# The first batch of an attention and expert kernel: the mask added by TensorE in PSUM instead of by VectorE, and a new order of that stage

## The chip, the cores and the metric

The kernel runs on one core of a Trainium2 chip. The metric is the time of one execution in device microseconds; for the kernel before it is the median of three runs. The profile is of one more execution of the same program, and its times count from the start of its span.

## The reference, cut to what matters

Four batches of attention with 8 heads, 576 positions and head size 64 feed two expert layers; the change is in the attention of batch 0.

```
scores = scale * np.matmul(q, k.transpose(0, 1, 3, 2))          # scale = 1 / 8
mask_plain = (rel >= 0) & (rel < 32)                            # heads 0 to 3
mask_dil = (rel >= 0) & (rel < 128) & (rel % 4 == 0)            # heads 4 to 7
scores = np.where(masks, scores, -1e9)
scores = scores - max(scores);  attn = exp(scores)
out = (attn / (sum(attn) + 1e-9)) @ v                           # (2304, 512) in all
x = max(out @ w1, out @ w2, out @ w3) @ w_out                   # moe, d_ff 768
...                                                             # moe2: 8 experts, d_ff 1024
```

## The kernel before, in words

The heads of a batch are done in four pairs, p = 0 to 3; pairs 2 and 3 are the dilated ones, with positions sorted so that their mask is a band too. For a pair the 576 query positions are nine tiles of 64; a tile's scores are 96 keys wide, and both heads of the pair stand above one another on 128 partitions. So a pair's scores are 128 x 864, in two PSUM banks of five and four tiles (480 and 384 columns).

A pair goes through steps, named by letters in a written order (`attn_ops`, from line 151): S computes the scores on TensorE (L181); Ma scales them and adds the mask on VectorE (L192), into SBUF (tile `sm`); Mb takes the maximum over each tile's keys, negated (L200). Pairs 0 and 2 are "fused": Xe is nine exponentials on ScalarE with the maximum as bias, each with its sum read out (L215). Pairs 1 and 3 aren't: Xs adds the maximum on GpSimd (L204), Xe is one exponential over 864 columns (L212), Xb sums on VectorE (L230). Ra adds 1e-9 to the sums and takes reciprocals (VectorE, L234 and L235), Rb multiplies by them (GpSimd, L238). T transposes the weights, three tiles in one group (TensorE, L249), E copies a group out of PSUM to SBUF (L253; a table says on ScalarE, A, or VectorE, V), V multiplies by v (TensorE, L266), one half at a time, H rounds the result to the first of two float parts (ScalarE, L286) and L subtracts to get the second (VectorE, L290). In a step's name the first digit is the pair, so T21 is group 1 of pair 2.

The inputs' weights `wm1` come as float64, as two 32-bit words, and are made into float32 by nine steps (`narrow_ops`, line 312): c1 takes the exponent (VectorE, L326), c2 moves it to its float32 place (ScalarE, L330), c3 puts the sign in (VectorE, L331), c4 masks the mantissa (VectorE, L334), c5 converts it (ScalarE, L337), c6 adds the low word (VectorE, L338), c7 multiplies (VectorE, L341), c8 rounds (ScalarE, L319), c9 subtracts (VectorE, L323). `g0`, `g1`, `g2` are 1 MB loads of such weights (L352), each worth two tiles of 512 columns. Here the second digit is the tile: c31 is c3 of tile 1. Tiles 0 and 1 come from `g0`, tile 2 from `g1`.

What sets the order: the loads of the stage go out on SP's queue in the order of `LOADS` (line 45; k is a pair's keys and queries, m a part of the mask, v the values, g weights). The steps follow `ORDER` (line 48) on every engine, each engine in order. Work that isn't in `ORDER` (the next weights, the gate's weights of `load_gate`, line 652, batch 1's loads) is put between by a scheduler at compile time. Batches 1 to 3 run later beside the expert layers by `STAGES` (line 42) and `LATE`, always fused; their TensorE work starts with L175, their VectorE work with L192. After the stage come the first expert layer's products (L419). The first batch's score tiles are in the pool `ps_a` for pairs 0 and 2 and in `ps_g` for pairs 1 and 3.

Of the kernel before, what the change touches and what calls it, by code (L numbers as in the profile page):

```python
# [9 lines left out]
F32 = mybir.dt.float32  # L10
# [31 lines left out]
STAGES = {0: "S Ma Mb Xs Xe Xb Ra Rb", 6: "W", 8: "T0 E0 T1 E1", 9: "T2 E2", 11: "V0 H0 L0 V1 H1 L1"}  # L42


LOADS = "k0 m0 k1 k2 m2 k3 v0 g0 v1 g1 v2 v3"
FUSED = "1010"
EVAC = "AAV VAA VAV AAA".split()
ORDER = (
# [52 lines left out]
def attention_moe(ctx: ExitStack, tc: tile.TileContext, q, k, v, mask, wm1, wg, wm2, out):  # L101
# [27 lines left out]
    mk = at_p.tile([P, BANK0 + NQ * KW], F32, name="mk", bufs=1)  # L129
# [21 lines left out]
    def attn_ops(b, p, pool, qt, kt, vt, fused, evac):  # L151
# [12 lines left out]
        def s():  # L164
            if b == 0 and p % 2:
# [14 lines left out]
            for t in range(0 if corners else NQ):  # L180
                nc.tensor.matmul(  # L181
                    h["s"][t // T0][:, (t % T0) * KW:(t % T0 + 1) * KW],
                    qt[:, t], kt[:, t * QT:t * QT + KW],
                    start=True, stop=True,
                )

        def ma():
            h["m"] = pool.tile([P, NQ, KW], F32, name="sm", bufs=2 if pool is at_p else 3)
            for a, (t0, t1) in enumerate(halves):
                n = (t1 - t0) * KW  # L190
                m0 = BANK0 + t0 * KW if dil else a * KW
                nc.vector.scalar_tensor_tensor(  # L192
                    out=h["m"][:, t0:t1].rearrange("p t k -> p (t k)"),
                    in0=h["s"][a][:, 0:n], scalar=1.0 / D ** 0.5, in1=mk[:, m0:m0 + n],
                    op0=ALU.mult, op1=ALU.add,
                )

        def mb():
            h["st"] = pool.tile([P, 3, NQ], F32, name="st")
            nc.vector.tensor_reduce(out=h["st"][:, 0], in_=h["m"], axis=AX.X, op=ALU.max, negate=True)  # L200

        def xs():
            if not fused:
                nc.gpsimd.tensor_tensor(  # L204
                    out=h["m"], in0=h["m"], in1=h["st"][:, 0].unsqueeze(2).to_broadcast([P, NQ, KW]),
                    op=ALU.add,
                )

        def xe():
            sm, st = h["m"], h["st"]  # L210
            if not fused:
                nc.scalar.activation(out=sm, in_=sm, func=AF.Exp)  # L212
                return
# [13 lines left out]

        def xb():
            if not fused:
                nc.vector.tensor_reduce(out=h["st"][:, 1], in_=h["m"], axis=AX.X, op=ALU.add)  # L230
# [61 lines left out]
        ops = {"W": w, "S": s, "Ma": ma, "Mb": mb, "Xs": xs, "Xe": xe, "Xb": xb, "Ra": ra, "Rb": rb}  # L292
# [19 lines left out]
    def narrow_ops(dst, bits, parts):  # L312
# [8 lines left out]
        def lo():  # L321
            for w, x in parts:
# [384 lines left out]
    for what in LOADS.split():  # L707
# [30 lines left out]
    assert not steps  # L738
    at0_p.release()
# [156 lines left out]
    def hooks(unit):  # L896
# [626 lines left out]
```

## Time and profile before

| what | us |
|---|---|
| median of three runs | 1898.69 (1898.12 to 1899.18) |
| the profiled execution, its own time | 1901.93 |
| its span in the trace | 1899.9 |
| TensorE busy | 1853.2 (98% of the span) |
| VectorE busy | 1341.1 (71%) |
| ScalarE busy | 976.6 (51%) |
| GpSimd busy | 651.3 (34%) |

In the profile PE is TensorE's matmuls and PEld its weight loads, DVE is VectorE, ACT ScalarE, POOL GpSimd, SPq the queue of SyncE that issues DMAs. A busy share is an average over the whole span. The first batch's stage takes the first 47 us of it.

### The profile page before, as it was taken

The page shows a single profiled execution, that of the slowest core. Times are in us where ns is not written, and L with a number is a line of the kernel's source. Part 1 is how long each engine was busy: PE and PEld are TensorE (multiplying, and loading weights), DVE is VectorE, ACT ScalarE, POOL GpSimd, SP SyncE. Part 2 cuts the span into 40 slices and gives each one's busy share as a digit, 9 for nine tenths or more (in the row PEclk, how much of TensorE's full clock was granted, in tenths as well). Part 3 has the DMA queues.
Part 4 walks back from the last instruction along what each step waited for, and adds up shares of the span by engine and source line. Part 5 has one row for each costly group of instructions (what it writes and reads, how often), then busy time and mean ns, then how long its engine had stood idle before and what let it go on. Part 6 is the DMA issues. An engine that isn't in the chain of part 4 may idle for free.

```text
span 1899.9 us, 34083 instructions
## 1 busy us (share of the span) xinstructions
PE 1853.2 (98%) x12051; PEld 1745.9 (92%) x12051; DVE 1341.1 (71%) x2529; ACT 976.6 (51%) x2362; POOL 651.3 (34%) x553
## 2 busy tenths in 40 slices
PE   7899999999999999999999999999999999999998
PEld 6899999998899987999999999999989999999997
DVE  7983364677866667666677777777777677876777
ACT  5663445444554444444456555565545555555554
POOL 2123243335666667666612121121211111211111
PEclk7899999999999999999999999999999999999999
DMA  7766486866667678766977767777798676676763
GB/s 262 277 217 222 151 274 202 304 226 228 237 252 259 252 252 291 263 254 250 363 257 235 237 218 225 239 233 237 232 331 262 211 233 225 225 255 212 234 219 100
DMA packets 218488, 458.81 MB, mean 241 GB/s; under 512 B 19920, under 2 KB 102992, under 8 KB 216784
## 3 DMA queue, kind: packets, MB, share of 16 engines
q1 hardware_dynamic: 216688, 454.29, 70.2%
q10 hardware_dynamic: 1632, 2.36, 0.4%
q8 instruction: 95, 1.56, 0.3%
q14 instruction: 73, 0.60, 0.1%
HBM read 325.76 MB, written 130.81 MB: 240 GB/s over the span
## 4 chain that ended last, share of the span: by engine, by line
PE 83%; DVE 8%; DMA 4%; ACT 2%; issue 1%; POOL 1%; DVEq 0%; SPq 0%; ACTq 0%; POOLq 0%
PE po L1292 25%; PE po L1387 12%; PE po L1037 10%; PE ps L419 7%; PE p L1387 6%; PE q L1387 6%; PE q L1083 4%; PE p L1083 4%; PE ps L629 4%; DMA raw<-in_wm 1%; PE ps L549 1%; DVE sums L771 1%; PE q L549 1%; DVE h L1135 1%; DVE ts L810 1%
## 5 line engine op out<-in xcount | busy, mean ns | idle before, releaser
L1292 PE MATMUL po<-wt,hop 128*128 128x256 f32 (+1 forms) x3264 | 482.9, 310 | 2.8 <-DMA wt<-wtd 2.8
L1292 PEld LDWEIGHTS po<-wt,hop 128*128 128x128 f32 x3264 | 444.9, 191 | 38.5 <-ACT wt L83 3.0
L84 POOL TENSOR_TENSOR wt<-raw,wt 128x256 fp32r<-128x256 f32 x192 | 186.2, 994 | 757.9 <-ACT wt L83 746.9
L84 DVE TENSOR_TENSOR hop<-r,hop 128x384 fp32r<-128x384 f32 x384 | 208.9, 574 | 188.3 <-ACT hop L83 184.7
L1037 PE MATMUL po<-wb,h 128*128 128x512 f32 x1152 | 295.2, 392 | 0.4 <-POOL wb L84 0.4
L1037 PEld LDWEIGHTS po<-wb,h 128*128 128x128 f32 x1152 | 213.6, 188 | 34.3 <-POOL wb L84 1.2
L83 ACT CAST hop<-r 128x384 fp32r<-128x384 f32 x384 | 188.7, 516 | 55.7 <-DVE r L1268 30.8
L419 PE MATMUL ps<-xt,wa 128*128 128x288 f32 x1296 | 187.7, 301 | 4.6 <-DVE wa L323 2.0
L419 PEld LDWEIGHTS ps<-xt,wa 128*128 128x128 f32 x1296 | 176.9, 191 | 8.2 <-DVE wa L323 2.3
L84 POOL TENSOR_TENSOR wa<-raw,wa 128x256 fp32r<-128x256 f32 (+1 forms) x107 | 129.8, 1217 | 111.9 <-ACT wa L83 91.0
L1401 ACT ACTIVATE r<-r 128x384 f32<-128x384 f32 x192 | 99.8, 525 | 128.9 <-DVE r L1400 128.0
L84 POOL TENSOR_TENSOR tw<-ts,tw 128x512 fp32r<-128x512 f32 x64 | 85.3, 1354 | 93.5 <-DVE h L1135 57.4
L1387 PE MATMUL po<-xB,wa 128*128 128x384 f32 x576 | 116.9, 338 | 0.0
L1387 PE MATMUL po<-xt,wa 128*128 128x384 f32 x576 | 116.9, 338 | 0.0
L1321 DVE SCALAR_TENSOR_TENSOR acc<-po,prob,acc 128x256 f32<-128x256 f32 x222 | 95.1, 476 | 21.9 <-PE po L1292 17.5
L84 POOL TENSOR_TENSOR wa<-sums,wa 128x512 fp32r<-128x512 f32 x64 | 88.7, 1404 | 53.3 <-ACT wa L83 28.4
L84 POOL TENSOR_TENSOR wb<-raw,wb 128x512 fp32r<-128x512 f32 x64 | 93.2, 1456 | 29.2 <-ACT wb L83 28.8
L1387 PEld LDWEIGHTS po<-xB,wa 128*128 128x128 f32 x576 | 102.5, 188 | 0.0
L1387 PEld LDWEIGHTS po<-xt,wa 128*128 128x128 f32 x576 | 102.5, 188 | 0.0
L1262 DVE TENSOR_TENSOR r<-r,r 128x384 f32<-128x384 f32 x128 | 93.1, 728 | 2.2
L771 DVE TENSOR_TENSOR sums<-raw 128x256 f32<-128x256 f32 x64 | 41.4, 646 | 71.1 <-DMA raw<-in_wm 71.1
L1303 ACT COPY mm<-po 128x256 f32<-128x256 f32 x144 | 49.6, 375 | 79.9 <-PE po L1292 79.9
(236 smaller groups left out, 3364.7 us busy)
## 6 DMA issues: line engine op xcount, KB each, us to landing
wa<-wsd SPq DMA_DIRECT2D x192, 512.0 KB, 4.4
wt<-wtd SPq DMA_DIRECT2D x256, 256.0 KB, 3.9
wsd<-wa SPq DMA_DIRECT2D x96, 512.0 KB, 3.4
raw<-in_wm SPq DMA_DIRECT2D x64, 512.0 KB, 4.3
wtd<-tw SPq DMA_DIRECT2D x128, 256.0 KB, 2.8
raw<-in_wm SPq DMA_DIRECT2D x128, 256.0 KB, 5.4
wa<-wsd SPq DMA_DIRECT2D x64, 256.0 KB, 4.7
cx<-in_wm SPq DMA_DIRECT2D x12, 1024.0 KB, 6.8
```

Of the source, the lines that this page charges most:

```text
L83: nc.scalar.copy(hi, src)
L84: sub.tensor_tensor(out=lo, in0=src, in1=hi.bitcast(F32), op=ALU.subtract)
L419: nc.tensor.matmul(ps, w[:, wi, kk], xt[:, xi, kk, n0:n0 + HB], start=(n == 0), stop=(n == 3 * KT - 1),)
L629: nc.tensor.matmul(ps, wo[f][:, wi, d2 * P:(d2 + 1) * P], hs[f][:, hi, a * HB:(a + 1) * HB], start=(f == 0 and n == 0), stop=(f == NF1 - 1 ...
L771: nc.vector.tensor_tensor(out=s[:, o], in0=x, in1=y, op=op)
L1037: nc.tensor.matmul(po, self.hs[f, j][:, hi, t * P:(t + 1) * P], self.ws[f][:, wi], start=(n + f + k == 0), stop=(n == NPAIR - 1 and f == 1 ...
L1083: nc.tensor.matmul(ps, wo[w][:, wi, kk], xo[x][:, xi, kk], start=(first and k == 0), stop=True if k == 5 else False, skip_group_check=not ...
L1262: nc.vector.tensor_tensor(out=r[o, n], in0=r[x, n], in1=r[y, n], op=op)
L1292: nc.tensor.matmul(self.ps[side, t][:, 0:x.shape[-1]], h[:, hi, t * P:(t + 1) * P], x, start=(first and i == 0), stop=(n == NPAIR - 1 and ...
L1321: nc.vector.scalar_tensor_tensor(out=a, in0=src, scalar=g, in1=a, op0=ALU.mult, op1=ALU.add)
L1387: nc.tensor.matmul(ps[k][side], wo[k][w][:, wi, kk], xo[x][:, xi, kk], start=(first and c == 0), stop=c == 5, skip_group_check=not first,)
L1401: nc.scalar.activation(out=r, in_=r, func=AF.Relu)
```

## The change

TensorE starts each bank of batch 0's scores with a matmul of 8 times the identity and the mask, and the score matmuls add to it. M then takes the maximum from PSUM, in two parts, and scales it by 1/8; X is nine exponentials that read PSUM, for all four pairs. Ma, Mb, Xs, Xe and Xb are gone from batch 0, Xs and Xb altogether. Only 64 partitions of the mask are loaded; its first part is copied to the matmul's type by ScalarE, its second by GpSimd (r2), and after the stage a DMA copies it to the other 64 partitions for later batches. The mask's first part is the first load, the gate's weights are loaded third, and `g0` stands ahead of pair 3's keys and queries. Pair 1's evacuations are all VectorE's, and pair 2's scores go to `ps_g` in place of pair 3's. c1 is one masking operation instead of a shift and a mask, with c2's factor to match. Batches 1 to 3 allocate their statistics tile in Ma rather than in Mb.

```diff
-STAGES = {0: "S Ma Mb Xs Xe Xb Ra Rb", ...
+STAGES = {0: "S Ma Mb Xe Ra Rb", ...
-LOADS = "k0 m0 k1 k2 m2 k3 v0 g0 v1 g1 v2 v3"
-FUSED = "1010"
-EVAC = "AAV VAA VAV AAA".split()
+LOADS = "m0 k0 w0 k1 k2 m2 g0 k3 v0 g1 v1 v2 v3"
+EVAC = "AAV VVV VAV AAA".split()
 ORDER = (
-    "S0 M0a S1 M0b X0s X0e M1a S2 M1b X1s M2a X0b M2b S3 X1e R0a X2s X2e X1b R0b M3a T01+1 R1a "
-    "T02 M3b R1b E01 c11 T00+2 c10 c21 X2b E02 X3s R2a c20 T12+1 c31 E00 c30 E12 T10+1 R2b X3e "
-    "c41 V01 c40 T11 E10 c51 V00 X3b c50 T22 E11 c12 H00 T21 R3a H01 V10 c61 c22 R3b E22 E21 "
-    "V11 H10 c32 T20 H11 c60 c71 T31 c42 E31 E20 c52 c70 L01 T30+1 L00 c81 T32 V20 c62 E30 c91 "
-    "E32 L10 V21 c80 L11 V30 H20 c72 H21 L20 V31 H30 L21 c90 H31 L30 c82 L31 c92"
+    "S0 M0 X0 S1 M1 r2 R0a R0b X1 S2 M2 c10 c11 T02+1 T01 E02 c20 c21 E01 R1a R1b T00+2 E00 S3 X2 "
+    "c30 c40 c31 V01 V00 M3 R2a R2b c41 c50 T10 T11 E10 E11 T12 E12 c51 H01 H00 V11 V10 c12 X3 c60 c70 c61 "
+    "c71 R3a R3b c22 L01 L00 T20 E20 T21 E21 T22 E22 c80 H11 c81 H10 V21 V20 c90 c32 c42 L11 L10 c91 "
+    "T30+1 E30 T31 E31 T32 E32 c52 H21 H20 c62 L21 c72 L20 V31 V30 H31 c82 H30 c92 L31 L30"
 )
...
-    mk = at_p.tile([P, BANK0 + NQ * KW], F32, name="mk", bufs=1)
+    mr = at_p.tile([P, BANK0 + NQ * KW], F32R, name="mk", bufs=1)
+    mk = mr.bitcast(F32)
+    mraw = at0_p.tile([QT, BANK0 + NQ * KW], F32, name="mraw", bufs=1)
+    eyes = const.tile([QT, P], F32R, name="eyes")
+    for c in range(0, P, QT):
+        nc.vector.tensor_scalar_mul(eyes[:, c:c + QT], ident[:QT, :QT], float(D ** 0.5))
...
+            for a, (t0, t1) in enumerate(halves if b == 0 else ()):
+                n, m0 = (t1 - t0) * KW, mask_at(a)
+                nc.tensor.matmul(
+                    h["s"][a][:, 0:n], eyes, mr[:QT, m0:m0 + n], start=True, stop=False, skip_group_check=True,
+                )
...
-                    start=True, stop=True,
+                    start=False, stop=True, skip_group_check=True,
...
+        def m():
+            weights()
+            for a, (t0, t1) in enumerate(halves):
+                nc.vector.tensor_reduce(
+                    out=h["st"][:, 0, t0:t1],
+                    in_=h["s"][a][:, 0:(t1 - t0) * KW].rearrange("p (t k) -> p t k", k=KW),
+                    axis=AX.X, op=ALU.max, negate=True,
+                )
+            nc.vector.tensor_scalar_mul(h["st"][:, 0], h["st"][:, 0], 1.0 / D ** 0.5)
+
+        def x():
+            for a, (t0, t1) in enumerate(halves):
+                for t in range(t0, t1):
+                    nc.scalar.activation(
+                        out=h["m"][:, t], in_=h["s"][a][:, (t - t0) * KW:(t - t0 + 1) * KW], func=AF.Exp,
+                        scale=1.0 / D ** 0.5, bias=h["st"][:, 0, t:t + 1], accum_out=h["st"][:, 1, t:t + 1],
+                    )
...
-                out=z, in0=high, scalar1=20, scalar2=0x7FF,
-                op0=ALU.logical_shift_right, op1=ALU.bitwise_and,
+                out=z, in0=high, scalar1=0x7FF00000, scalar2=None, op0=ALU.bitwise_and
             ),
-            "c2": lambda: nc.scalar.activation(out=z, in_=z, func=AF.Relu, scale=2.0 ** 23, bias=ebias),
+            "c2": lambda: nc.scalar.activation(out=z, in_=z, func=AF.Relu, scale=8.0, bias=ebias),
...
-            nc.sync.dma_start(mk[:, m0:m1], mask[:, m0:m1])
+            nc.sync.dma_start(mraw[:, m0:m1], mask[:QT, m0:m1])
+            if i == 0:
+                nc.scalar.copy(mr[:QT, m0:m1], mraw[:, m0:m1])
+        elif what[0] == "w":
+            nc.sync.dma_start(wgr, wg)
...
+    steps = {"r2": lambda: nc.gpsimd.tensor_copy(mr[:QT, BANK0:], mraw[:, BANK0:])}
...
+    nc.sync.dma_start(mk[QT:, :], mk[:QT, :])
```

## Rows read from the trace of the kernel before

**Rows 1.** The page's first part: busy us, share, instructions.
```profile
PE 1853.2 (98%) x12051; PEld 1745.9 (92%) x12051; DVE 1341.1 (71%) x2529; ACT 976.6 (51%) x2362; POOL 651.3 (34%) x553
```
**Rows 2.** Busy time by stretch: length; busy per engine; clock, DMA share, GB/s.
```profile
7.07:20.37 13.30, 10.12 (x71) 9.45 (x71) 10.37 (x17) 7.96 (x38) 3.94 (x3) 0.87 1.03 358
20.37:47.25 26.88, 18.29 (x196) 15.06 (x196) 26.81 (x52) 17.63 (x38) 7.82 (x5) 0.68 0.65 212
47.25:90.00 42.75, 36.34 (x350) 33.76 (x349) 42.75 (x65) 27.42 (x74) 4.30 (x2) 0.88 0.74 272
90.00:120.00 30.00, 27.34 (x313) 25.86 (x312) 28.21 (x49) 24.32 (x75) 4.04 (x2) 1.00 0.66 231
```
**Rows 3.** The chain of waits, first 62 us: start, us, what.
```profile
1.19 4.04 DMA qt<-in_q
...
5.25 9.98 DMA qt<-in_q
...
20.46 2.92 DVE raw L326 x2
...
57.22 1.85 PE ps L419 x12
```
**Rows 4.** The issue of the first weights' load at 7.6 us, and its landing.
```profile
L352 SPq DMA_DIRECT2D cx<-in_wm x1: 347/347/347, 7.6 to 7.6; - x1
...
DMA to landing us min/median/max: 12.0/12.0/12.0
```
**Rows 5.** Groups by form, first 48 us: busy us, mean ns | idle before, releasers.
```profile
L238 POOL TENSOR_TENSOR sm<-sm,st 128x864 f32<-128x864 f32 x4 | 7.1, 1764 | 8.3 <-DVE st L235 7.4 <-ACT sm L212 0.9
L215 ACT ACTIVATE sm<-sm,st 128x96 f32<-128x96 f32 x18 | 6.5, 360 | 7.6 <-DVE st L200 7.6
...
L331 DVE SCALAR_TENSOR_TENSOR raw<-cx,raw 128x512 uint32<-128x512 uint32 x4 | 4.9, 1250 | 0.0
...
L200 DVE TENSOR_REDUCE st<-sm 128x9 f32<-128x864 f32 x4 | 4.2, 1040 | 0.1
...
L326 DVE TENSOR_SCALAR raw<-cx 128x512 uint32<-128x512 uint32 x4 | 3.7, 976 | 0.0
...
L338 DVE SCALAR_TENSOR_TENSOR cx<-cx 128x512 f32<-128x512 uint32 x4 | 2.7, 668 | 0.0
...
L319 ACT CAST wa<-raw 128x512 fp32r<-128x512 f32 x4 | 2.5, 627 | 0.0
...
L253 DVE COPY pt<-pst 96x384 f32<-96x384 f32 x4 | 2.2, 546 | 0.0
...
L334 DVE TENSOR_SCALAR cx<-cx 128x512 uint32<-128x512 uint32 x4 | 1.6, 415 | 0.0
...
L192 DVE SCALAR_TENSOR_TENSOR sm<-ps,mk 128x480 f32<-128x480 f32 x2 | 1.3, 658 | 1.0 <-PE ps L181 0.9
...
L192 DVE SCALAR_TENSOR_TENSOR sm<-ps,mk 128x384 f32<-128x384 f32 x2 | 1.1, 558 | 1.3 <-PE ps L181 1.3
...
L234 DVE TENSOR_SCALAR st<-st 128x9 f32<-128x9 f32 x4 | 0.6, 159 | 0.0
```
**Rows 6.** GpSimd's instructions in order of time: start, us, what [idle before].
```profile
19.69 1.63 POOL L238 TENSOR_TENSOR sm<-sm,st 128x864 f32<-128x864 f32 x1 [2.35 <-DVE st L235]
21.28 1.81 POOL L204 TENSOR_TENSOR sm<-sm,st 128x864 f32<-128x864 f32 x1
```
**Rows 7.** VectorE's instructions in order of time.
```profile
7.07 0.66 DVE L192 SCALAR_TENSOR_TENSOR sm<-pss,mk 128x480 f32<-128x480 f32 x1 [6.07 <-PE pss L181]
...
46.57 0.68 DVE L323 TENSOR_TENSOR wa<-raw,wa 128x512 fp32r<-128x512 f32 x1
...
51.78 1.12 DVE L192 SCALAR_TENSOR_TENSOR sm<-pss,mk 128x384 f32<-128x384 f32 x2
```
**Rows 8.** L266 alone in two stretches: length, PE and PEld busy, clock, DMA, GB/s.
```profile
30.84:33.03 2.19, 2.19 (x36) 2.00 (x36) 0.50 0.72 204
36.03:37.30 1.27, 1.27 (x36) 1.13 (x36) 1.00 0.64 255
```

More of the change, by code (lines that the diff above doesn't have):

```diff
@@ L41 @@
 }
-STAGES = {0: "S Ma Mb Xs Xe Xb Ra Rb", 6: "W", 8: "T0 E0 T1 E1", 9: "T2 E2", 11: "V0 H0 L0 V1 H1 L1"}
-LOADS = "k0 m0 k1 k2 m2 k3 v0 g0 v1 g1 v2 v3"
-FUSED = "1010"
-EVAC = "AAV VAA VAV AAA".split()
+STAGES = {0: "S Ma Mb Xe Ra Rb", 6: "W", 8: "T0 E0 T1 E1", 9: "T2 E2", 11: "V0 H0 L0 V1 H1 L1"}
+LOADS = "m0 k0 w0 k1 k2 m2 g0 k3 v0 g1 v1 v2 v3"
+EVAC = "AAV VVV VAV AAA".split()
 ORDER = (
[5 rows of a table removed]
[4 rows of a table added]
 )
@@ L149, in keep_warm, with attn_ops @@
             nc.tensor.matmul(ps, ident[:, :ps.shape[0]], ident, start=True, stop=True)
-    def attn_ops(b, p, pool, qt, kt, vt, fused, evac):
+    def attn_ops(b, p, pool, qt, kt, vt, evac):
         if p == 0 and b < 3:
@@ L164, in s @@
         def s():
-            if b == 0 and p % 2:
+            if b == 0 and p in (1, 2):
                 h["s"] = [ps_g.tile([P, 512], F32, name="ps") for _ in range(2)]
@@ L183, in s, with mask_at, weights @@
                     qt[:, t], kt[:, t * QT:t * QT + KW],
-                    start=True, stop=True,
+                    start=False, stop=True, skip_group_check=True,
                 )
+        def mask_at(a):
+            return BANK0 + halves[a][0] * KW if dil else a * KW
+        def weights():
+            h["m"] = pool.tile([P, NQ, KW], F32, name="sm", bufs=2 if pool is at_p else 3)
+            h["st"] = pool.tile([P, 3, NQ], F32, name="st")
+        def m():
[14 more added lines that the diff above has]
+                    )
         def ma():
-            h["m"] = pool.tile([P, NQ, KW], F32, name="sm", bufs=2 if pool is at_p else 3)
+            weights()
             for a, (t0, t1) in enumerate(halves):
-                n = (t1 - t0) * KW
-                m0 = BANK0 + t0 * KW if dil else a * KW
+                n, m0 = (t1 - t0) * KW, mask_at(a)
                 nc.vector.scalar_tensor_tensor(
@@ L198, in mb @@
         def mb():
-            h["st"] = pool.tile([P, 3, NQ], F32, name="st")
             nc.vector.tensor_reduce(out=h["st"][:, 0], in_=h["m"], axis=AX.X, op=ALU.max, negate=True)
[L202 to L207, printed above, removed]
         def xe():
             sm, st = h["m"], h["st"]
-            if not fused:
-                nc.scalar.activation(out=sm, in_=sm, func=AF.Exp)
-                return
             for t in range(NQ):
@@ L226, in xe_part @@
                 )
-        def xb():
-            if not fused:
-                nc.vector.tensor_reduce(out=h["st"][:, 1], in_=h["m"], axis=AX.X, op=ALU.add)
         def ra():
@@ L290, in lo @@
                 nc.vector.tensor_tensor(out=y, in0=src, in1=x.bitcast(F32), op=ALU.subtract)
-        ops = {"W": w, "S": s, "Ma": ma, "Mb": mb, "Xs": xs, "Xe": xe, "Xb": xb, "Ra": ra, "Rb": rb}
+        ops = {"W": w, "S": s, "M": m, "X": x, "Ma": ma, "Mb": mb, "Xe": xe, "Ra": ra, "Rb": rb}
         for i in range(5):
@@ L714, in attention_moe @@
             m0, m1 = (0, BANK0) if i == 0 else (BANK0, BANK0 + NQ * KW)
-            nc.sync.dma_start(mk[:, m0:m1], mask[:, m0:m1])
+            nc.sync.dma_start(mraw[:, m0:m1], mask[:QT, m0:m1])
[3 more added lines that the diff above has]
+            nc.sync.dma_start(wgr, wg)
         else:
             raws[i] = fetch_w1(0, i)
-    steps = {}
+    steps = {"r2": lambda: nc.gpsimd.tensor_copy(mr[:QT, BANK0:], mraw[:, BANK0:])}
     for p in range(H // 2):
-        fused = FUSED[p] == "1"
-        for name, op in attn_ops(0, p, pools[p], *qk[p], vs[p], fused, EVAC[p]).items():
-            if name not in ("W", "X0", "X1", "X2", "X3", "X4"):
+        for name, op in attn_ops(0, p, pools[p], *qk[p], vs[p], EVAC[p]).items():
+            if name not in "W X0 X1 X2 X3 X4 Ma Mb Xe".split():
                 steps[f"{name[0]}{p}{name[1:]}"] = op
@@ L933, in hooks @@
                     ahead[b, p] = attn_ops(
-                        b, p, at_p, *load_qk(b, p, at_p), None, True, "AAA"
+                        b, p, at_p, *load_qk(b, p, at_p), None, "AAA"
                     )
```

1 line of the change is left out of this document (removed).

## The prediction

> **What bounds the kernel now.** I read the page's first part, then the busy time by stretch, the chain of waits, and the first 48 us engine by engine. Over the span TensorE is the full engine [rows 1], but that average hides the opening, where the change lies. From 20.37 to 47.25 us VectorE is busy 26.81 of 26.88 us and from there to 90 us without a gap, while TensorE has room; from 90 us on both are nearly full and TensorE takes over [rows 2]. So an edit of the first batch pays by when VectorE gets through the stage, and what it saves there should reach the end as a shift: behind it stand only fixed work of VectorE, then of TensorE.
>
> Three things are to be seen before 47 us. The chain enters with DMAs: pair 0's q lands at 5.23 and pair 3's at 15.23, then VectorE follows VectorE [rows 3]. The first pair of weights (`g0`) lands only at 7.6 + 12.0 = 19.6 [rows 4], and its first operation, c1, starts at 20.46 [rows 3]. And VectorE's busy time isn't all work. c1 (L326) takes 976 ns at 128x512 where c4 (L334), also one source and a scalar, takes 415; c3 (L331) takes 1250 where c6 (L338) takes 668 [rows 5]. The two c1 that fill 20.46 to 23.38 lie beside two GpSimd operations from 19.69 to 23.09 [rows 3, 6]: one waits out the other. That is 3.7 - 1.6 = 2.1 us in c1 and 4.9 - 2.7 = 2.2 us in c3, 4.3 us of VectorE lost. Its operations on PSUM don't show it (the evacuations stay at 546 ns).
>
> **The change part by part**, on VectorE's clock from its first maximum at 7.07 to the stage's last c9 at 47.25 [rows 7].
>
> *Its work.* Eight additions of the mask go, 4 x (0.66 + 0.56) = 4.88 us, four maxima from SBUF, 4 x 1.04 = 4.16, and two sums (as L200 in kind and shape), 2.08: 11.1 us [rows 5]. In come, per pair, two maxima from PSUM and a multiplication of nine columns. No row is a maximum from PSUM; the nearest are L192, which reads PSUM at these two widths (0.66 and 0.56), and below them L200, whose 1.04 us for 864 columns would make 0.6 and 0.5 by width. I take the upper, nearer one, and 0.16 for the small operation: 1.38 a pair, 5.5 in all. Pair 1's two evacuations that move from ScalarE cost 2 x 0.55 = 1.1. Sum: -11.1 + 6.6 = **-4.5 us**, to -5.0 with the lower price.
>
> [...] The rows price VectorE's reads of PSUM and SBUF alike: from L192's two widths it pays 1.04 ns a column plus 0.16 us, and L200 from SBUF 0.14 us beside its columns. [...] No two rows of ScalarE differ in the source alone; I give its exponentials today's pitch and take nothing for it.
>
> *The lock between VectorE and GpSimd.* The two shifts by the maximum on GpSimd go. Four multiplications (L238) stay, and in the new order pair 0's lies beside a maximum from PSUM, pair 2's beside pair 1's evacuations and pair 3's beside L01, L00, E20, all with PSUM. Only pair 1's still meets a c3: it runs from about 16.1 to 17.7 and the c3 is ready near 16.4, 1.3 us lost. **-3.0 us**; if all collide as now, 0.
>
> *The head.* The mask's first part is now issued before pair 0's k and q, so q is issued one slot (0.47 us) later and lands near 5.6. The mask, 120 KB, lands before that, and its copy on ScalarE (L319 takes 0.63 us for 512 columns [rows 5]) is done by then. Between the later start and c1, VectorE has three maxima and little else. `g0` now stands ahead of pair 3's loads and 0.3 MB of mask is saved, so at the 0.34 MB/us between pair 3's q and `g0` (1.5 MB in 4.4 us) [rows 3, 4] it lands near 14.7 and pair 3's q near 17.4. VectorE idles some 3.5 us there, against 13.30 - 10.37 = 2.9 now. With the start: **+0.8 us**, from 0.3 to 1.5.
>
> *New waits.* VectorE is now behind ScalarE's queue, where every pair now has nine exponentials, 9 x 0.36, some 3.3 us (so far two pairs; the others have one operation). From 9.0 that queue runs X0, X1, two c2, two evacuations, X2 to 21.2 and X3 to 26.7, with little idle. VectorE's c3 waits for c2 (0.6), its reciprocals for X2 (0.9) and X3 (0.4), E22 for a transpose (0.5), and pair 2's c6 for a c5 behind three evacuations (1.9): 4.3 us. Behind each waits all that VectorE has in order, and the TensorE transposes on its evacuations. About 5.5 us of later weights' work now runs inside the stage and can fill all but the first gap; I let it fill 60% of 3.7, so **+2.1 us** is left, between 0.6 and 4.3.
>
> *At nothing.* Eight matmuls for the mask: the nearest of that type is L419, 1.85 us for 12 of 288 columns [rows 3], 0.26 us at 480; the far bound is a few times that. They go before q arrives and in TensorE's gaps; if pair 2's doesn't, up to 1 us. GpSimd's copy of the mask's second part stands ahead of pair 0's multiplication and is cheaper than that (1.76 us); it is done before X0 unless the mask lands late, then up to 1 us. The gate's load takes one issue slot ahead of pair 1, whose exponentials wait for ScalarE anyway. The copy of the mask to the upper partitions goes behind the stage in SP's queue; first needed at 51.78 [rows 7]. Without that slack its transfer (344 KB, about 1 us at the rates above) and SP's stores and loads behind it are exposed. The new c1 and c2 keep shape and engine: 0.
>
> Sum: -4.5 - 3.0 + 0.8 + 2.1 = **-4.6 us**. The profiled execution took 1901.93 us (1899.9 its span), 3.2 above the median of 1898.69; it would take 1897.3, and the median **1894.1 us**, or 0.24% less.
>
> **The rivals.**
>
> *More of the gaps fill.* Now VectorE idles 0.07 us after 20.37 [rows 2] though it waits on the same engines: later weights fill everything. If so after, 1.5 us more comes back, and with the lower price of the maximum 0.5: gain 6.6, 1892.1.
>
> [...]
>
> *Pair 3's loads too late: slower.* They are moved behind 1 MB of weights. M3 stands in VectorE's order ahead of R2a, a c4 and pair 1's evacuations; it ends some 3.5 us after q. With q at 17.4 that is 20.9, when X2 has 0.3 us left; every us past that stops all of VectorE for as much. From q at 22.3 the gain is gone, from 26.1 the kernel is over 0.2% slower. For it: four loads and `g0` share one queue, and `g0` itself took 12 us. Against: what lies ahead of pair 3 is 4.9 MB, 0.7 more than now. It would give 1903.
>
> *Not what it says, or hidden anyway:* the mask surely leaves VectorE. Were it not the bound after the stage, nothing would change: 1898.7; its unbroken stretch to 90 us speaks against that.
>
> **How the numbers follow.** My forecast, gain 3.8 to 6.0: 0.42. More filling: 0.20. The tail's clock or empty gaps: 0.27. No change: 0.05. Slower: 0.06. So faster by over 0.2% 0.62, within 0.32 (0.27 + 0.05), slower 0.06. The range takes in both first rivals, the upper price of each unknown and no change: 1890.0 to 1899.0; the forecast's own is 1892.7 to 1894.9.
>
> **What would show it.** Right: `g0`'s c1 near 15 us; c1 and c3 of the stage near 0.4 and 0.67 us, but one c3 near 2; the last c9 near 42 instead of 47.25; every later landmark 5 us earlier. Wrong: pair 3's scores after 20 us, VectorE idle over 3 us in all between 20 us and the stage's end, a gain at 45 us that is gone at 120, or maxima from PSUM well over 0.66 us.

## The result, and the profile after

The changed kernel is slower: 1910.2 us (median of 4, 1908.55 to 1911.38) against 1898.4 (4 runs beside them), ratio 1.0061, 95% interval [1.0044, 1.0079]. The forecast was 1894.1, and the range ended at 1899. Its profiled execution took 1908.55 us, span 1906.8.

Three landmarks on TensorE tell where: the first scores of batch 1 came at 57.21 us instead of 47.50 (+9.7), the last product of batch 1's attention at 127.88 instead of 117.48 (+10.4), the first down matmul (the first expert layer's product with `w_out`) at 162.30 instead of 151.87 (+10.4). So nearly all of it arises in the first batch's stage; behind it is a shift.

Busy time by stretch, kernel before and then after, cut at 20 us and at batch 1's first scores (columns as in [rows 2]):

```profile
0.00:20.00 20.00, 15.19 (x96) 14.55 (x96) 10.17 (x19) 9.04 (x39) 4.74 (x10) 0.91 0.93 325
20.00:47.50 27.50, 18.76 (x198) 15.18 (x197) 27.43 (x52) 18.08 (x39) 8.19 (x5) 0.68 0.66 216
```
```profile
0.00:20.00 20.00, 13.86 (x75) 12.29 (x76) 4.19 (x13) 8.11 (x39) 3.90 (x10) 0.88 0.91 283
20.00:57.21 37.21, 23.19 (x224) 18.23 (x223) 29.27 (x63) 23.16 (x73) 5.16 (x3) 0.68 0.74 208
57.21:90.00 32.79, 28.93 (x310) 26.65 (x309) 31.47 (x50) 23.36 (x64) 1.73 (x2) 0.96 0.75 269
```

VectorE (third pair) was idle 9.83 us of the first 20 and 0.07 behind; now it is idle 15.81 and 7.94. That is 13.85 us more idle against 4.14 less busy: +9.71, the whole delay. Its work did shrink as foreseen. Groups by form, first 62 us, against [rows 5]:

```profile
L347 DVE SCALAR_TENSOR_TENSOR raw<-cx,raw 128x512 uint32<-128x512 uint32 x4 | 3.2, 800 | 0.0
...
L343 DVE TENSOR_SCALAR raw<-cx 128x1024 uint32<-128x1024 uint32 x3 | 2.1, 694 | 4.5 <-DMA cx<-in_wm 4.5
...
L343 DVE TENSOR_SCALAR raw<-cx 128x512 uint32<-128x512 uint32 x4 | 1.6, 419 | 2.5 <-DMA cx<-in_wm 2.5
L205 DVE TENSOR_REDUCE st<-ps 128x5 f32<-128x480 f32 x2 | 1.3, 658 | 7.7 <-PE ps L189 7.7
...
L205 DVE TENSOR_REDUCE st<-ps 128x4 f32<-128x384 f32 x2 | 1.1, 559 | 1.3 <-PE ps L189 1.3
```

c1 (L343) takes 419 ns instead of 976 and c3 (L347) 800 instead of 1250: 3.8 us of lock with GpSimd are gone. The maxima from PSUM (L205) take 658 and 559 ns, just the price of the additions they replace. But the idle column has grown: 7.7 us for these scores (0.9 before), and, new, 2.5 and 4.5 for weights' loads (`cx<-in_wm`). In order of time on VectorE, against [rows 7]:

```profile
12.75 0.21 DVE L252 RECIPROCAL st<-st 128x9 f32<-128x9 f32 x1
18.90 0.66 DVE L205 TENSOR_REDUCE st<-ps 128x5 f32<-128x480 f32 x1 [5.94 <-PE ps L189]
20.61 0.56 DVE L205 TENSOR_REDUCE st<-ps 128x4 f32<-128x384 f32 x1 [1.05 <-PE ps L189]
...
21.28 0.75 DVE L343 TENSOR_SCALAR raw<-cx 128x512 uint32<-128x512 uint32 x2
...
25.86 0.43 DVE L343 TENSOR_SCALAR raw<-cx 128x512 uint32<-128x512 uint32 x1 [2.48 <-DMA cx<-in_wm]
...
33.37 0.68 DVE L354 SCALAR_TENSOR_TENSOR cx<-cx 128x512 f32<-128x512 uint32 x1
38.16 0.69 DVE L343 TENSOR_SCALAR raw<-cx 128x1024 uint32<-128x1024 uint32 x1 [4.11 <-DMA cx<-in_wm]
38.77 0.68 DVE L357 TENSOR_TENSOR raw<-raw,cx 128x512 f32<-128x512 f32 x1
39.37 0.17 DVE L251 TENSOR_SCALAR st<-st 128x9 f32<-128x9 f32 x1
```

The wait that ends at 18.90 is for pair 2's scores. The one at 25.86 belongs to the second weight group's second half (tile 3), the one at 38.16 to the third group (`g2`). Neither is in the written order: the compiler put them between. Behind the last one stand tile 1's c7 (c71) and pair 3's reciprocal (39.37), whose exponentials had ended at 33.2, and with them all four pairs' ends. TensorE and SP in order of time:

```profile
9.62 2.22 PE L189 MATMUL ps<-kt,qt 128*128 128x96 f32 x18 [0.60 <-DMA qt<-in_q]
15.40 1.09 PE L175 MATMUL ps<-mk,eyes 64*128 64x480 f32 x2 [3.56 <-POOL mk L737]
16.42 4.15 PE L189 MATMUL ps<-kt,qt 128*128 128x96 f32 x18
```
```profile
16.77 0.35 SPq L140 DMA_DIRECT2D kt<-in_k  x1
17.62 0.35 SPq L141 DMA_DIRECT2D qt<-in_q  x1
20.48 0.33 SPq L368 DMA_DIRECT2D cx<-in_wm  x1
```

Pair 2's scores wait for GpSimd's copy of the mask's second part, whose load was issued at 4.83 and landed 9.6 us later; then TensorE, idle for 3.56 us before, takes 4.15 us for 18 matmuls instead of 2.22, at granted clock 0.50. TensorE alone, over pair 1's scores and over pair 2's (length; busy; granted clock; DMA share, GB/s):

```profile
9.62:11.84 2.22, 2.22 (x18) 1.00 1.10 295
16.42:20.57 4.15, 4.15 (x20) 0.50 1.06 252
```

And `g2`'s load is issued at 20.48, behind batch 1's k and q, where the kernel before issued it at 13.10, ahead of them; it lands at 38.2 instead of 32.4. SP's queue in the kernel before:

```profile
13.10 0.35 SPq L352 DMA_DIRECT2D cx<-in_wm  x1
15.31 0.35 SPq L137 DMA_DIRECT2D kt<-in_k  x1
```

The chain of waits, against [rows 3], says the same: no VectorE operation holds it until 38 us.

```profile
1.99 4.09 DMA qt<-in_q
...
6.87 13.59 DMA qt<-in_q
...
20.48 17.66 DMA cx<-in_wm
...
38.16 0.69 DVE raw L343
```

Two more things are on SP. The chain has `g2`'s issue (20.48) right behind the landing of pair 3's q (6.87 + 13.59 = 20.46), so the late loads of the head held it too, not its place alone. And the mask's copy to the upper partitions, meant to go behind the stage, was issued at 21.95 and landed 17.1 us later, beside `g2`'s load. No run moved that copy by itself, so its share isn't shown.

### The profile page after: what moved, and what is told of

The parts are those of the page before. It is cut to its first block, busy times and chain, and to the rows that moved or that the text cites. A ratio compares the mean times of both kernels' runs of the same rounds, so it can differ in the third digit from the quotient of the medians.

```text
span 1906.8 us, 34127 instructions
## 1 busy us (share of the span) xinstructions
PE 1853.9 (97%) x12055; PEld 1744.0 (91%) x12055; DVE 1329.6 (70%) x2531; ACT 979.0 (51%) x2395; POOL 646.1 (34%) x552
## 4 chain that ended last, share of the span: by engine, by line
PE 83%; DVE 8%; DMA 4%; ACT 2%; issue 1%; POOL 1%; SPq 0%; DVEq 0%; ACTq 0%; POOLq 0%
PE po L1311 25%; PE po L1406 12%; PE po L1056 9%; PE ps L435 8%; PE p L1406 6%; PE q L1406 6%; PE q L1102 4%; PE p L1102 4%; PE ps L645 4%; DMA cx<-in_wm 2%; DMA raw<-in_wm 2%; PE ps L565 2%; PE q L565 1%; DVE h L1154 1%; DVE ts L829 1%
## 5 line engine op out<-in xcount | busy, mean ns | idle before, releaser
L1340 DVE SCALAR_TENSOR_TENSOR acc<-po,prob,acc 128x256 f32<-128x256 f32 x222 | 95.1, 476 | 20.3 <-PE po L1311 17.6
L790 DVE TENSOR_TENSOR sums<-raw 128x256 f32<-128x256 f32 x64 | 39.4, 616 | 74.9 <-DMA raw<-in_wm 74.9
```

What stands on the lines that cost most here:

```text
L1340: nc.vector.scalar_tensor_tensor(out=a, in0=src, scalar=g, in1=a, op0=ALU.mult, op1=ALU.add)
```

## The experiments

The theories: A, the mask's late second part holds pair 2's scores and with them VectorE's queue. B, put-in weight work stands in VectorE's order ahead of the stage's own and waits for loads that land late. C, the stage's own chain (ScalarE's exponentials, transposes, products) is the bound, with under 1.5 us to be had from e1. D came up on the way and is told in e4's expectation, E ahead of e16's. All kernels but e10 and e11 are edits of the changed kernel. The landmarks, from TensorE's timeline, with VectorE's idle time up to batch 1's first scores:

| run | ratio to before [95%] | scores b1 | last product | first down | idle |
|---|---|---|---|---|---|
| before | 1 | 47.5 | 117.5 | 151.9 | 9.9 |
| after | 1.0061 [1.0044, 1.0079] | 57.2 | 127.9 | 162.3 | 23.8 |
| e1 | 1.0056 [1.0039, 1.0074] | 59.6 | 131.9 | 166.3 | 23.9 |
| e2 | 1.0029 [1.0017, 1.0042] | 55.6 | 126.8 | 161.2 | 19.5 |
| e3 | 1.0036 [1.0021, 1.0052] | 50.6 | 122.6 | 157.0 | 15.7 |
| e5 | 1.0014 [1.0002, 1.0027] | 47.0 | 118.1 | 153.8 | 19.2 |
| e6 | 1.0038 [1.0026, 1.0050] | 44.8 | 121.9 | 156.3 | 17.2 |
| e7 | 1.0036 [1.0023, 1.0049] | 45.9 | 124.2 | 158.6 | 18.5 |
| e8 | 1.0016 [1.0008, 1.0025] | 50.6 | 121.1 | 155.5 | 21.7 |
| e4 | 1.0053 [1.0041, 1.0065] | 56.7 | 128.7 | 163.1 | 19.3 |
| e9 | 1.0035 [1.0022, 1.0048] | 46.4 | 123.1 | 157.4 | 18.9 |
| e9b | 1.0023 [1.0012, 1.0033] | 45.3 | 118.4 | 154.3 | 17.6 |
| e10 | 0.9997 [0.9989, 1.0006] | 47.8 | 116.6 | 152.5 | 10.2 |
| e12 | 1.0057 [1.0044, 1.0070] | 56.2 | 127.1 | 161.5 | 20.8 |
| e13 | 1.0022 [1.0010, 1.0034] | 46.4 | 124.0 | 158.4 | 20.8 |
| e14 | 1.0067 [1.0050, 1.0084] | 54.4 | 127.7 | 162.0 | 20.2 |
| e15 | 1.0032 [1.0020, 1.0044] | 48.7 | 123.7 | 159.7 | 21.1 |
| e11 | 1.0009 [1.0000, 1.0018] | 47.0 | 120.7 | 155.1 | 9.5 |
| e16 | 1.0028 [1.0019, 1.0037] | 51.7 | 118.8 | 153.2 | 16.8 |
| e17 | 1.0013 [1.0004, 1.0022] | 50.3 | 116.8 | 153.8 | 19.3 |

Landmarks are of one execution each, and from the first down matmul to the end an execution took 1743 to 1752 us, so that they are read with the ratios, not for them.

### Loads or order: e1, e2, e3, e5

e1, the third group's load listed behind `v3`:
```diff
-LOADS = "m0 k0 w0 k1 k2 m2 g0 k3 v0 g1 v1 v2 v3"
+LOADS = "m0 k0 w0 k1 k2 m2 g0 k3 v0 g1 v1 v2 v3 g2"
```


> The changed kernel with one edit: the third load of weights (g2) is written at the end of the list of loads, so that it goes out ahead of batch 1's keys and queries, as it did before the change. [...] A, the mask: pair 2's scores wait for the late second part of the mask (15.4 us), and everything of VectorE behind its maximum with them; this edit leaves that alone, so the time stays within 1.5 us of the changed kernel's. B, the put-in work: the compiler placed the first step of later weights (tile 3 from g1, all of g2) in VectorE's order where it expected their loads, they land later, and all behind waits (2.48 us at 25.9, 4.11 us at 38.2): g2 then lands near 33 to 35, the wait of 4.1 us goes, and the total falls by 3 to 4.5 us. [...]

e2, the mask's second part straight behind pair 0's loads; e3 is both edits:
```diff
+LOADS = "m0 k0 m2 w0 k1 k2 g0 k3 v0 g1 v1 v2 v3"
```


> The changed kernel with one edit: the mask's second part is the fourth load, ahead of the gate's weights and pair 1's keys and queries, in place of the ninth. [...] B, the put-in work: the head is earlier all the same, but VectorE then stands at the same two loads (25.8 and 38.1), so the total falls by less than 1.5 us. C: under 1.5 us.

> Both edits together: the mask's second part fourth, and g2 written at the end of the list of loads. A alone right: as with the mask's edit alone, 3 to 5 us. B alone right: as with g2's edit alone, 3 to 4.5 us. Both right, one hiding the other: 6 to 9 us less than the changed kernel, that is 1901 to 1904. C: under 2 us.

e5, no edit of loads: VectorE's put-in work of tile 3 and of `g2` may stand in its order only behind the listed c72.
```diff
+            with tc.issue_after(held) if g == 2 else ExitStack():
                 op()
...
+            held = made_by.ins if name == "c72" else held
...
+    with tc.issue_after(held):
         for op in narrow_ops(raw[:, 1], t[:, 1024:2048], [(first_w[3], raw[:, 1])]).values():
```


> The changed kernel with one edit: VectorE's steps of tile 3 and of g2's weights may not stand in its order ahead of pair 2's tile's c7, so none of the put-in work is met before the stage's end. B, the put-in work: both waits for loads go, batch 1's first scores (57.2 us in the changed kernel) start before 53, and the total falls by 3 to 5 us, the later weights' own 5.5 us being done behind the stage. A and C: batch 1's first scores not before 56, the total within 1.5 us or higher, as the gaps of the stage are left empty.

e5 gave back most of the loss (1.0014) with the mask as late as ever. VectorE's waits that are left in its first 46 us, beside those for pair 0's and 1's scores:

```profile
18.27 0.66 DVE L205 TENSOR_REDUCE st<-ps 128x5 f32<-128x480 f32 x1 [5.13 <-PE ps L189]
19.98 0.56 DVE L205 TENSOR_REDUCE st<-ps 128x4 f32<-128x384 f32 x1 [1.05 <-PE ps L189]
38.56 0.69 DVE L354 SCALAR_TENSOR_TENSOR cx<-cx 128x512 f32<-128x512 uint32 x1 [1.03 <-ACT cx L353]
43.53 0.69 DVE L343 TENSOR_SCALAR raw<-cx 128x1024 uint32<-128x1024 uint32 x1 [1.39 <-DMA cx<-in_wm]
```

The last of them is for the load of the group behind `g2`, which isn't held. So C isn't what delays the stage to 57.2: the same chain, with only an order on VectorE set, ends 10.2 us earlier (47.0). Of these, 4.5 us are less idle time and 5.7 are weight work that now comes later; up to the last product it is 6.2 and 3.6 of 9.8. A is a smaller part by the landmarks, 1.6 us at batch 1's scores in e2; by its ratio e2 gave half, some 6 us where A had 3 to 5, and the two readings aren't reconciled. e1 alone settled nothing; all loads of that execution were late (pair 1's q at 12.0), and `g2`, though issued ahead of batch 1's k and q, landed at 37.5 and was waited for. In e3 it landed at 31.7, and batch 1's scores came 6.6 us earlier than in the changed kernel (50.6), but the ratio is no better than e2's: the forecast for both causes missed.

### Both causes together: e8, e6, e7, e4

e8 is e5 with the hold on `g2` alone; e6 is e5 and e2, e7 these and e1; e4 loads the mask on 128 partitions (`mask[:, m0:m1]` for `mask[:QT, m0:m1]`) and uses the lower 64.

> The changed kernel with the hold on the third weight group's work alone; the fourth tile's work may stand where the compiler puts it, as in the changed kernel. Theory B splits: the third group's load lands last (38.2 us; 4.1 us of visible wait), the fourth tile's 25.8 (2.5 us of visible wait). If the waits are what each costs: the ratio falls from 1.006 to 1.003, 5 to 6 us of the 9 that both holds gave. If the third group's work is the one that stands in the way of everything listed behind it: it gives all 9, ratio 1.0015. If the fourth tile's is: it gives under 3, ratio 1.005.

> The changed kernel with two edits: the work put in from the later weights (VectorE's operations of the first batch's fourth weight tile and of the third weight group) may stand in VectorE's order only behind the listed c72, and the mask's second part is loaded straight behind pair 0's q and k. Theory B with A (put-in work blocks VectorE; and the late second part of the mask holds pair 2's scores, 5.1 us of VectorE's wait in the run with the hold alone): the wait at pair 2's maxima falls from 5.1 us to under 2.5, no wait for a weight load over 1.5 us is left before 44 us, and the first scores of batch 1 come at 43 to 45 us (47.0 with the hold alone); the ratio to the kernel before is 0.998 to 1.000. Theory A alone (the mask is the whole cause): the hold adds nothing to the early mask, and the ratio stays at the 1.003 that the early mask gave. If the loads as a whole are the bound (the queue's rate sets the stage): the wait moves from pair 2's maxima to c10 or to pair 3's scores, in the same size, and the ratio stays at 1.0014.

> As the run before, and the third group's load issued behind v3, ahead of batch 1's q and k. Theory B: with the hold the third group's work stands behind c72, at some 40 us; its load landed at 38 us in the changed kernel, so that an earlier load gives at most the 1.4 us of wait that the hold left at 43.5 us, and takes as much from batch 1's q and k (their landings move by 2.5 us, from 32 and 33 to 35 and 36, still ahead of 43): the ratio is within 0.001 of the run before. If batch 1's first scores wait for their q after all: slower than the run before by 1 to 2 us.

> The changed kernel with the mask's two parts loaded on all 128 partitions, as the kernel before loads them (the lower 64 rows unused), nothing else. In the changed kernel the second part's packets, to 64 partitions, took 230 ns each at the median, 135 in the kernel before, and it landed 9.6 us after its issue (8.3 before). If loading 64 partitions slows the queue (a theory of its own, D): the second part lands by 13.2 us instead of 14.4 though it moves twice the bytes, and VectorE's wait at pair 2's maxima falls from 5.9 to under 5. If bytes set it: it lands 0.5 to 1 us later, the wait grows to 6.5 to 7, and the ratio is 1.006 to 1.007. Theory B: in either case the ratio stays within 0.001 of the changed kernel's 1.0061.

e8: the hold on `g2` alone gave 1.0016, as good as both by the ratio; `g2` is the one in the way. e6 and e7 missed: at 1.0038 and 1.0036 they are no better than the early mask alone. The first stage did end earlier (44.8 us), but the second took 77.1 us to its last product instead of 70.0. In e6 TensorE has the last pair's scores ready as early as in the kernel before, and VectorE's addition of its mask comes 6.7 us later (1.3 before: scores at 92.21, addition at 93.54):

```profile
92.97 1.04 PE L183 MATMUL pss<-kt,qt 64*64 64x96 f32 x36
```
```profile
99.66 1.12 DVE L224 SCALAR_TENSOR_TENSOR sm<-pss,mk 128x384 f32<-128x384 f32 x2
```

Between them stands put-in work and work of the first expert layer, again in the compiler's order. With the early mask the mask's copy also went out ahead of batch 1's k and q (14.78 in e6), so these edits move more than one load, and why the second stage is longer isn't shown. e4: twice the bytes landed earlier, 8.4 us behind its issue (13.3 us for 14.4), and the wait for pair 2's scores fell from 5.94 to 2.08, as theory D has it. But VectorE then waited 4.68 us for tile 3's load, and no gain reached the end that can be told from noise (1.0053), as B has it.

### How much the put-in work costs: e9, e9b, e10, e12

e9 is e6 with the second and third group of output weights held behind batch 1's last L; e9b holds the first as well; e10 is that hold in the kernel before; e12 lists `c10 c11` ahead of `M2`.
```diff
+            behind = held if g == 2 else lows[1, 3, 1] if g > NG else None
+            with tc.issue_after(behind) if behind else ExitStack():
                 op()
```


> The hold and the early mask together, and VectorE's work of the second and third group of output weights (needed only by the first down matmul, some 30 us later) held behind the last L operation of batch 1's attention. The account on VectorE up to the last attention matmul of batch 1, from the groups by form: kernel before 118.0 us of work (72.5 of it put-in weight work) at 117.5 us; hold alone 109.2 (68.2 put in) and 8.9 idle, at 118.1; hold and early mask 115.9 (74.2 put in) and 6.0 idle, at 121.9. Theory B in its wider form (both attention stages are bound by VectorE's order; what the compiler puts in ahead of the attention's own work is paid in full, and time that a shorter wait sets free is taken by more put-in work): the four operations of the second output group that stand ahead of the stage's end, 3.8 us, go behind it; the last attention matmul comes at 117.5 to 118.5 us, the first down matmul at 152 to 153 (156.3), the ratio falls from 1.0038 to 1.0015 to 1.002. If the second stage is set by TensorE and the attention's own chain: nothing changes, 1.0038.

> As the run before, with the first group of output weights held as well. Theory B in its wider form: 6 to 7.5 us more of put-in work leave the stage, the last attention matmul comes at 111 to 113 us; then VectorE has some 25 us of held work and 10 of the up matmuls' in the 34 us to the first down matmul: that comes at 146 to 149 us, ratio 0.997 to 0.999. Rival: the held work is late for the down matmuls, and what the stage gains is lost there: the first down matmul at 152 or later, ratio over 1.001.

> The kernel before with the three groups of output weights held in the same way, and nothing of the change. Theory B in its wider form: the put-in work that leaves the stage (one operation of each of two kinds of the second group and all of the first, 8 to 9 us) is paid there too: the last attention matmul at 109 to 111 us instead of 117.5, the first down matmul at 144 to 147 instead of 151.9, ratio 0.996 to 0.998. If only the changed kernel is bound by what is put in: ratio 1.000.

> The changed kernel with c10 and c11 listed ahead of pair 2's maxima in place of behind them. In the changed kernel VectorE waits 5.9 us for pair 2's scores, to 18.9, and c10's weights had landed at 16.7. Theory A: the two operations (0.43 us each) fall into the wait, the first stage is 0.9 us shorter, and c2 and c3 of these tiles start 4 us earlier: ratio 1.004 to 1.0055. Theory B: the put-in work takes the time back, or its waits on loads stand at the same absolute times (25.9 and 38.2 us): ratio 1.0055 to 1.0065. If the weights come later than the scores: slower by up to 1 us.

The wider form of B fell. In e10 VectorE did 6.0 us less weight work before the last product (66.5 for 72.5, sums of the groups by form), and that came 0.9 us earlier, with 3.0 us more idle; the end didn't move. e9 missed too, and e9b got 3.4 us of the 9 or more that it was to give, and came out as its rival has it: the first down matmul at 154.3, 35.9 us behind the last product instead of 34.4. So put-in work isn't paid us for us, and putting it off is not what made e5 fast: what costs is put-in work that waits. e12 moved the first stage by 1.0 us and the time by nothing that can be told; its `g2` landed 0.8 us earlier (37.35), so that even the 1.0 us need not be its edit's.

### The load itself: e13, e14, e15, e11

e13 is e9 with every hold set later (`g2` and tile 3 behind the first batch's last L, groups 7 and 8 and the first output group behind the last pair's maxima); e15 is e9b with the mask as in the changed kernel; e11 loads the gate's weights third in the kernel before, as the change does. e14 puts a copy of 1 MB that nobody reads ahead of `g2`'s load:
```diff
+        if g == 2:
+            junk = dram.tile([P, 2, 1024], U32, name="junk")
+            nc.sync.dma_start(junk, wm1[g].bitcast(U32))
```


> The early mask, and all put-in work held behind the attention's own: the fourth tile's and the third group's operations on VectorE behind the last L of the first batch, those of the eighth weight group and of the first two output groups that stand ahead of the last pair's maxima of batch 1 behind these maxima or, for the second and third output group, behind that batch's last L. Theory B: no wait for a weight load is left in the first stage (e9: 1.7 us at 43 us, and 2.9 for ScalarE ahead of it), its first batch-1 scores at 41 to 43 us (46.4 in e9), the last pair's maxima operation 3 to 6 us earlier against its scores (7.3 us behind them in e9); the last attention matmul at 117 to 120 (123.1), ratio 1.000 to 1.002. If the time is lost elsewhere (the second stage is set by TensorE and the later weights' own due times): the last attention matmul at 122 or later, ratio 1.003 or more.

> The changed kernel with one cost doubled, nothing else: a copy of 1 MB that nobody reads stands on SP's queue straight ahead of the third weight group's load (landed 38.2 us in the changed kernel, waited for since 34.1). As built, the work that the compiler puts into VectorE's order ahead of the first stage's last L is the same as in the changed kernel. Theory B: the load lands 2.5 to 4 us later, VectorE's wait for it grows from 4.1 to 6.5 or more, the first scores of batch 1 come at 59.5 to 61.5 us (57.2), ratio 1.007 to 1.0085. Theories A and C (the mask, or the stage's own chain): the wait grows, the stage does not; ratio within 0.0005 of 1.006.

> The run with the hold alone (ratio 1.0014, last attention matmul at 118.1 us with 68.2 us of put-in work ahead of it), with the three groups of output weights held as well; the mask as in the changed kernel. If put-in work is paid in full in the second stage: 4.5 us less of it, the last attention matmul at 113.5 to 115, ratio 0.999 to 0.9995. If, as in the kernel before (6 us less of it gave 0.9), the second stage has another bound close by: the last attention matmul at 117 to 118, ratio 1.001 to 1.002.

> The kernel before with one part of the change alone: the gate's weights (16 KB, 128 packets of 128 bytes) loaded behind pair 0's q and the mask's first part in place of behind batch 1's q. The loads behind it (the second pair's q landed at 9.0 us, the mask's second part at 12.3) shift by the time its packets take, 0.1 to 0.5 us; VectorE is never idle behind 20 us there, so that little of it reaches the end: ratio 0.9995 to 1.0007. If this small load is what slows the changed kernel's queue (its loads landed 1 to 3 us later from the second q on): landings 1 us or more later, ratio 1.001 to 1.002.

e14 missed B's forecast and is inconclusive: its interval holds the changed kernel's ratio; the load landed at 39.4, 1.2 us later, but VectorE waited only 0.56 for it, since the compiler had set its c1 behind more work, and batch 1's first scores came 2.8 us earlier (54.4) where B had them 2 to 4 us later. e13 and e15 missed. Of these four e11 told most: a load of 16 KB moved, and the compiler's order on SP changed: `g2` behind batch 1's k and q there too, landing at 33.6 for 32.4. So the order alone doesn't make the 5.8 us of the changed kernel. VectorE had other work till then and waited for no load from 20 to 90 us, and the kernel is at most 0.18% slower.

### TensorE's clock: e16, e17

Theory E: it is TensorE's pace in the head that delays the first stage. Pair 2's 18 score matmuls took 4.13 to 4.16 us in 10 of the 15 profiled executions of changed kernels so far (in the changed kernel 4.15, behind 3.56 us idle, at granted clock 0.50), and those of pairs 0 to 2 took 2.22 to 2.56 in the three of the kernel before. e16 is the changed kernel with dummy matmuls (three more at the start, seven ahead of pair 2's scores), e17 the same in e8.
```diff
+            if b == 0 and p == 2:
+                keep_warm(h["s"][0][:, 0:P], 7)
...
-    keep_warm(ps_g.tile([P, 512], F32, name="ps")[:, 0:P], 8)
+    keep_warm(ps_g.tile([P, 512], F32, name="ps")[:, 0:P], 11)
```


> [...] Here the changed kernel with dummy matmuls only: three more at the start, seven ahead of pair 2's scores, in the time in which TensorE waits. The put-in work ahead of the first stage's last L and of batch 1's last L is as in the changed kernel. Theory E: pair 2's scores take 2.2 to 2.5 us, VectorE's maxima of pair 2 end by 19.5 us (21.2), batch 1's first scores come at 53 to 55 (57.2), ratio 1.003 to 1.0045. Theory B: the later waits stand at the landings of the weights (25.9 and 38.2 us), whatever comes before them: first scores of batch 1 at 56 to 57.5, ratio 1.005 to 1.0065.

> [...] With the waits on the loads away, theories B and E together say that the earlier scores now reach the end of the stage: first scores of batch 1 at 47 to 49 us (50.6), the last attention matmul at 118 to 119.5 (121.1), ratio 0.9995 to 1.001. If the head's clock doesn't reach the end of the stage: 1.0016 again. If the dummies delay pair 0's scores by more than the clock gives: 1.002 or more.

e16 came out just beyond E's forecast (1.0028 for 1.003 to 1.0045, first scores at 51.7 for 53 to 55), but not for E's reason. Its SP and VectorE in order of time:

```profile
15.89 0.35 SPq L370 DMA_DIRECT2D cx<-in_wm  x1
16.79 0.35 SPq L140 DMA_DIRECT2D kt<-in_k  x1
18.71 0.33 SPq L141 DMA_DIRECT2D qt<-in_q  x1
```
```profile
24.95 0.43 DVE L345 TENSOR_SCALAR raw<-cx 128x512 uint32<-128x512 uint32 x1 [2.27 <-DMA cx<-in_wm]
...
31.52 0.68 DVE L356 SCALAR_TENSOR_TENSOR cx<-cx 128x512 f32<-128x512 uint32 x1
32.71 0.69 DVE L345 TENSOR_SCALAR raw<-cx 128x1024 uint32<-128x1024 uint32 x1 [0.51 <-DMA cx<-in_wm]
33.32 0.68 DVE L359 TENSOR_TENSOR raw<-raw,cx 128x512 f32<-128x512 f32 x1
33.92 0.17 DVE L253 TENSOR_SCALAR st<-st 128x9 f32<-128x9 f32 x1
```

From pair 3's maxima (25.29 us, 27.14 in the changed kernel) to 42 us VectorE's order is the changed kernel's, row for row, but the compiler issued `g2` ahead of batch 1's k and q again. It landed at 32.7 instead of 38.2, the c1 started at 32.71 instead of 38.16 (-5.45), and batch 1's first scores came at 51.74 instead of 57.21 (-5.47): one for one. That is the experiment that e14 was to be, met by chance and not by design. It doesn't stand alone: in e3 and e12 too these scores come 18.8 us behind `g2`'s c1, with c1 at 31.76 and 37.35 (19.05 in the changed kernel; 19.7 and 22.0 in e4 and e1; 15 to 16 in e2 and e14, where more work stands ahead of that c1). The head's clock is seen too: pair 2's scores took 2.25 us, at a mean granted clock of 1.00 over the first 20 us (0.88 in the changed kernel), and its maxima were done 3.1 us sooner (18.3 for 21.4); but VectorE then waited for tile 3's load to 24.95, 1.85 us were left at pair 3's maxima, and with `g2` landing at 38.2 the next wait would have taken these too. That the clock matters only once the loads don't, as B says, is argued from these rows; no run shows it by itself. e17, where `g2` is also issued ahead of batch 1's k and q (16.10), gave nothing that can be told from e8: its last product is ahead of the kernel before (116.8), its first down matmul, 37.0 us behind that instead of 34.4, is not.

No kernel with the change beats the kernel before; e5, e8 and e17 come nearest, 2.5 to 3 us above it by their ratios.

## Why the prediction was wrong

**Its work and the lock: right.** The sum had -4.5 and -3.0. VectorE's work other than on weights fell from 20.2 to 15.9 us up to batch 1's first scores (-4.3), with the maxima at the price taken, 1.38 a pair; the lock gave -3.8. That one slow c3 (1190 ns) was left agrees with the forecast by luck: the one foreseen was beside pair 1's multiplication, this one is put-in work (tile 3's), at 29.91 beside pair 2's (28.93 to 30.56).

**The failed step is "New waits".** It let "about 5.5 us of later weights' work" that "now runs inside the stage" fill 60% of the gaps, leaving +2.1 us, at most 4.3. The amount was near: 4.1 us more of it ran there (groups of weight work 22.4 us, against 22.1 of which 3.8 more were lock). But it doesn't move into a gap at run time. The compiler has fixed its place in VectorE's order, and there it waits for its load with the stage's work behind it: 2.48 and 4.11 us in sight. e5 and e8 (this work held back), and e16 (the load earlier, the stage as much earlier) show it. The account: -4.3 - 3.8 + 4.1 + 13.85 more idle = +9.8, against +9.7 measured.

**The load that was moved without being listed.** The sum prices the new places of the mask, the gate's load and `g0` on SP's queue, and says nothing of `g2`, which isn't in `LOADS`. It went behind batch 1's k and q and behind the late loads of the head, and its landing set the end of the stage. The mask's copy, put at nothing because it "goes behind the stage in SP's queue", went inside it (21.95).

**The head was mis-sized.** +0.8 (0.3 to 1.5) was the term, with "up to 1 us" if the mask's second part came late. VectorE idled 6.0 us more in the first 20. The estimate took 0.34 MB/us for the loads; in 10 to 20 us the queue moved 294 GB/s where it had moved 348, `g0` landed at 16.7 (14.7) and pair 3's q at 20.5 (17.4). The mask landed at 14.4, and pair 2's scores paid for it twice, by the wait (3.56 us of TensorE) and by the clock (4.15 us at 0.50). e2 and e6 show that this part is real at the first stage's end (1.6 us against the changed kernel, 2.2 against e5); that most of it is hidden while the weights' loads are late is argued from e16's rows.

**The rivals.** The slower one had the right side and the wrong load: pair 3's q at 20.5 was inside the margin worked out for it (22.3), and its maxima waited for nothing; by SP's queue it did hold `g2`. The 0.27 for the tail's clock or empty gaps was in part for a stage ended by TensorE's chain with its last products at the lower granted clock, 0.9 us more each by [rows 8] (2.19 us at 0.50, 1.27 at 1.00), 1896.6 in all by an estimate from these. The tail's clock wasn't the cause: the four products took 7.1 us, 7.2 before. Of the four signs named as wrong, two came true: pair 3's scores at 24.1 us, and VectorE idle for 7.9 us behind 20.

**Reads of PSUM.** ScalarE's nine exponentials of pair 0, now from PSUM and with a scale, start 0.317 us apart (the first at 9.33 us, the ninth at 11.87), 43 ns less than the 0.36 from SBUF before (9.65 to 12.53); those of the other pairs are as far apart (pair 1's 12.74 to 15.28). That is 0.4 us of ScalarE a pair, for which the prediction took nothing. VectorE's 658 and 559 ns at 480 and 384 columns are 1.03 ns a column and 0.16 us besides, against 0.14 from SBUF [rows 5] if a column costs as much there: an estimated 20 ns more.

**What stays open.** Why the best holds still lose 2 to 3 us. VectorE is idle 15.7 us or more up to batch 1's first scores in all changed kernels, against 9.9; with the holds less weight work is done by then, and that the second stage pays for a part of it is a guess. A written order for that stage wasn't tried. Open too is how the 5.8 us of `g2`'s later landing split between its place, the head's late loads and the mask's copy.

## What to carry to other kernels

Where a compiler fills an in-order engine's queue with later work, ask of each such operation which load it waits for and what stands behind it: time that is freed on the engine can go into such waits. Moving one load on a queue can reorder those that nobody listed, so read the issue order of the new build before costing the change. And look for the saved work and the new idle time apart: here the one came as worked out (-8 us), and the other was 13.9 us.

## What was not expected of the hardware

TensorE's pace in the head: in e8 the 18 score matmuls of pair 0, behind an idle gap of 1.70 us, take 3.29 us instead of 2.22, and those of pairs 1 and 2 4.15 each, at granted clock 0.50. A pair with its two mask matmuls (1.09 for 0.66) needs 5.1 us, which then paces the head. A gap before the scores doesn't decide it alone: behind 1.27 us (e9) they took 2.22 and behind 1.91 (e2) 2.44, and in e1, e12 and e15 pair 0's took 4.15 with no such gap. Nor does the granted clock tell it alone: in these three it is 1.00 all through the first 24 us, and what slowed their scores isn't shown.

```profile
7.77 3.29 PE L189 MATMUL pss<-kt,qt 128*128 128x96 f32 x18 [1.70 <-DMA qt<-in_q]
10.98 1.09 PE L175 MATMUL ps<-mk,eyes 64*128 64x480 f32 x2
12.00 4.15 PE L189 MATMUL ps<-kt,qt 128*128 128x96 f32 x18
16.09 1.09 PE L175 MATMUL ps<-mk,eyes 64*128 64x480 f32 x2
17.10 4.15 PE L189 MATMUL ps<-kt,qt 128*128 128x96 f32 x18
```

Half the partitions, so half the bytes, was no faster load here: behind the same loads the mask's second part took 8.8 to 9.7 us to land on 64 partitions, in five executions (9.6 in the changed kernel and e14, 9.7 in e15, 8.8 in e16, 9.0 in e17), and 8.4 on 128, in one (e4).
